# Two transformer layers on one core: block 0's attention logits are exchanged through DRAM in four quarters instead of two halves

## The chip, the cores and the metric

The kernel runs on one core of one Trainium2 chip. The metric is the device time of one execution in microseconds. A core has a matrix engine (TensorE, PE in the profile; PEld is its weight load), a vector engine (VectorE, DVE), a scalar engine (ScalarE, ACT), a general engine (GpSimd, POOL) and a queue engine (SyncE, SP). Transfers between DRAM and on-chip memory are issued from SP, ACT and POOL and are then carried by the core's 16 DMA engines. Each engine works through its own list of instructions strictly in order, and waits on semaphores where an instruction needs another engine's result.

## The reference

The input x is 2048 tokens by 1024 features, bf16. Two layers are applied twice each, alternating, every one with a residual:

```
x = x + A(layernorm(x))      # layer 0
x = x + B(layernorm(x))      # layer 1
x = x + A(layernorm(x))      # layer 2
x = x + B(layernorm(x))      # layer 3
```

A is a dilated sliding-window attention: 32 heads of 32 features, and each token attends to itself and to the tokens 2, 4, ... 14 places earlier, 8 positions in all.

```
qkv    = x @ wqkv                                  # 1024 x 3072
logits = einsum("bhsd,bhswd->bhsw", q, kg) / sqrt(32)   # kg: k shifted by 0, 2, ..., 14
attn   = softmax(where(in range, logits, -1e9))
o      = einsum("bhsw,bhswd->bhsd", attn, vg) ;  A = o @ wo
```

B is a gated unit with hidden width 3584: `h = relu(x @ W_gate) * (x @ W_up)`, then `h @ W_down`.

## The kernel before

The tokens are cut into four blocks of 512 (b = 0 to 3), each of four tiles of 128. TensorE does nothing but the matrix products, in an order that the Python code writes out: `proj(0,b)` (q, k, v of layer 0, block b), `wo(L,b)` (the output product of the attention), `plan_gu` and `plan_down` (the gated unit). Weights come in slabs of 1024 x 512 through a ring of five slots. Every product accumulates in one of eight PSUM banks, and ScalarE or VectorE copies it out.

The order on the other engines comes from a planner, the class Plan. Every step is put at a planned time (`plan.at`, `plan.on_dve`, `plan.chain`), the steps are sorted by that time, and the program is emitted in that order. The planned times only set the order; at run time each engine starts an instruction when its waits are over. The work of VectorE for the attention is one long chain (`plan.chain`), and other VectorE work is slipped in between its links by its due time.

All attention except its matrix products is VectorE work, and it needs two layouts. The projections give features on the 128 partitions and tokens along the row; the attention wants 32 heads x 4 token tiles on the partitions. So q, k and v travel through DRAM (`q_d`, `k_d`, `v_d`; loads L540, stores L404 and L407) and come back as `qhm`, `khm`, `vhm`. Block 0 of layer 0 does this differently for its logits (function `first_logits`, L450 to L529). There q and k stay in the feature layout (`q_fm`, `k_fm`), with the columns of the weights picked so that one partition holds one feature group of one head. For each of the eight chunks c of 128 features the code multiplies q with the shifted k (`mul`, L488, all eight shifts at once for c = 0 to 3) and adds the product to a sum in f32 (`add`, L499). After that the 4 partitions of each head still have to be added up. For this the sums go through DRAM: `turn(h)` stores the sums of four shifts, `lacc`, to `l_d` (L505), and loads them back as `lhm` with the four partitions of a head side by side in one row (L511); `fold(h)` (L525, L526) adds the four up into `L`. For c = 4 to 7 the chunks are done for the first four shifts (h = 0) and then for the last four (h = 1), so that the first half can travel while the second is computed.

After the second fold come the mask (L579), the maximum and its subtraction (L581 to L584), the exponential on ScalarE (L587), the normalisation (L592 to L597), and eight groups of products with v (L605 to L615), each stored by POOL to `o_d` (L616). When all eight are stored, SP loads `oT` from `o_d` (L624), and TensorE can start `wo(0,0)` (L684). In TensorE's order `wo(0,0)` stands behind the first group of the second half of q of block 3 (the hook `("q", 1, 0)`, L793).

Around this chain stands other work of block 0's time. `late_ln(0, 3, 70.0, on_vector=True, norm_at=78.0)` (L846) puts the layer norm statistics of block 3 on VectorE (bn_stats L224, bn_aggr L247); POOL takes the power (L257), ScalarE applies it (L264) and SP issues the transposing DMA into `xnT` (L270). The `xnT` tiles, the two `lacc` and one of the `lhm` tiles share a pool of four buffers (`tpose`, tag "T"); the other `lhm` shares one buffer with `q_fm` and `qhm` (`hm_pool`, tag "q"). Block 3's x is loaded in two DMAs (L837, `n = 2`), and the slabs of `wo` in one DMA each (L676).

On SP the order in the stretch from 59 to 107 us is: vhm part 1, transpose of block 2 (first half), vhm part 2, transpose of block 2 (second half), store of `lacc0`, vhm part 3, load of `lhm0`, vhm part 4, store of `lacc1`, load of `lhm1`, transpose of block 3 (first half), qhm part 1, transpose of block 3 (second half).

Of the kernel before, what the change touches and what calls it, by code (L numbers as in the profile page):

```python
# [30 lines left out]
NG = DH // DG  # L31
FG = P // H


# [6 lines left out]
def _ap(t, off, dims):  # L41
    return bass.AP(tensor=t.tensor, offset=t.offset + off, ap=[list(t.ap[0])] + [list(d) for d in dims])
# [81 lines left out]
def kernel(  # L124
# [11 lines left out]
    nc = tc.nc  # L136
# [11 lines left out]
    wo_v = A_wo.rearrange("(kc p) n -> p kc n", p=P)  # L148
# [6 lines left out]
    dram = ctx.enter_context(tc.tile_pool(name="dram", bufs=1, space=bass.MemoryType.DRAM))  # L155
# [143 lines left out]
    class First:  # L299
# [46 lines left out]
        def turn(self, t):  # L346
            self.tp[t] = [psum.tile([P, KC // 2, P], BF16, tag="acc", name="tp") for h in range(2)]
            for c in range(KC):
                nc.tensor.transpose(self.tp[t][c // 4][:, c % 4, :], self.xn[:, t, c * P:(c + 1) * P], ident[:])
# [100 lines left out]
    def first_logits(st, tm):  # L450
        hold, ready = {}, {}
        now = lambda: 0.0

        def begin():
            hold["q"] = hm_pool.tile([P, KC, BLK], BF16, tag="q", name="q_fm")
            hold["k"] = hm_pool.tile([P, KC, HALO + BLK], BF16, tag="k", name="k_fm")
            nc.gpsimd.memset(hold["k"][:, :, 0:HALO], 0.0)

        def evict(nm, c, acc, t):
            def f():  # L460
                if nm == "q":
# [21 lines left out]
        def mul(c, h):  # L483

            def f():
                w, n = (0, W) if h is None else (W // 2 * h, W // 2)
                pr = at_pool.tile([P, n, BLK], BF16, tag="pr", name=f"prod_{c}", bufs=2)
                nc.vector.tensor_tensor(pr[:], _ap(hold["q"], c * BLK, [[0, n], [1, BLK]]),  # L488
                                        _ap(hold["k"], c * ROW + HALO - DIL * w, [[-DIL, n], [1, BLK]]), op=ALU.mult)
                for i in range(2) if h is None else (h,):  # L490
                    hold[("pr", c, i)] = pr[:, W // 2 * i - w:W // 2 * (i + 1) - w].rearrange("p w (q t) -> p w q t", q=TPB)
            return f

        def add(c, h):
            def f():
                if c == 1:
                    hold[("acc", h)] = tpose.tile([P, TPB, W // 2, P], F32, tag="T", name=f"lacc{h}")
                acc = hold[("acc", h)][:].rearrange("p q w t -> p w q t")
                nc.vector.tensor_tensor(acc, hold[("pr", 0, h)] if c == 1 else acc, hold[("pr", c, h)], op=ALU.add)  # L499
            return f  # L500

        def turn(h):

            def store():
                nc.sync.dma_start(l_d[h].rearrange("q p w t -> p q (w t)"),  # L505
                                  hold[("acc", h)][:].rearrange("p q w t -> p q (w t)"))

            def load():
                pool, tag = ((tpose, "T"), (hm_pool, "q"))[h]
                hold[("l", h)] = pool.tile([P, FG, W // 2, P], F32, tag=tag, name=f"lhm{h}")  # L510
                nc.sync.dma_start(hold[("l", h)][:].rearrange("p a w t -> p (a w t)"),  # L511
                                  l_d[h].rearrange("q (h a) w t -> (q h) (a w t)", a=FG))
# [7 lines left out]
        def fold(h):  # L520
            def f():
                if h == 0:
                    st["L"] = at_pool.tile([P, W, P], F32, tag="L", name="L_0_0")
                l = hold[("l", h)]
                nc.vector.tensor_tensor(l[:, 0:2], l[:, 0:2], l[:, 2:4], op=ALU.add)  # L525
                nc.vector.tensor_tensor(st["L"][:, 4 * h:4 * h + 4, :], l[:, 0], l[:, 1], op=ALU.add)  # L526
            return f

        return {"evict": evict}  # L529
# [143 lines left out]
        return st  # L673

    def plan_wo(L, b, st, done):
        ws = [slab(wo_v[:, :, h * SLAB:(h + 1) * SLAB], f"wo_{L}_{b}_{h}", 30.0) for h in range(2)]  # L676
        hold = {}

        def mms(half, t):
            def f():  # L680
                acc = psum.tile([P, BLK], F32, tag="acc", name="acc_wo")
                hold[(half, t)] = acc
                for c in range(KC):
                    nc.tensor.matmul(acc[:], lhsT=st["oT"][:, c, t, :], rhs=ws[half]["t"][:, c, :],  # L684
                                     start=(c == 0), stop=(c == KC - 1))
            return f

        def add(half, t):
            def f():
                xs = x_tiles[b * TPB + t][:, half * SLAB:(half + 1) * SLAB]  # L690
                nc.vector.tensor_tensor(xs, hold.pop((half, t))[:], xs, op=ALU.add)
            return f

        wo_start.append((L, b, plan.pe, st["tm"]))
        st["wo_at"] = plan.pe
        for t in range(TPB):
            for half in range(2):
                e = plan.on_pe(8, mms(half, t), [ws[half]])
                plan.on_dve(e + T_EV, 0.7, add(half, t), done[t] if half == 1 else None)
# [203 lines left out]
```

## Time and profile before

| | us |
|---|---|
| median of 3 runs | 1619.19 (1618.88 to 1619.46) |
| the profiled execution | 1619.48 |
| its span, first to last instruction | 1617.7 |
| TensorE busy in it | 1610.6 |
| VectorE busy | 1057.0 |
| ScalarE busy | 440.7 |
| POOL busy | 124.9 |
| granted TensorE clock | 1.0 throughout |

The page of the profile lists busy time, a picture of the span in 40 slices, the DMA queues, the chain of work that ended last, and the costliest groups. Beside it stand views that list, for a stretch of time, every instruction of an engine with what ended its idle time ("the timeline"), who waited for whom ("the waits"), and the chain that ended last in order of time. In all of them the columns are start, duration, engine, line of the kernel, operation and tiles; a bracket holds the idle time before and who ended it. For a DMA the duration is that of its issue; its landing comes later.

### The profile page before, as it was taken

To read this page: it belongs to the slowest core of one execution; us is meant where nothing else is said; L and a number is where in the kernel's file an instruction comes from. 1 tells how busy PE (TensorE), PEld (TensorE's weight loads), DVE (VectorE), ACT (ScalarE), POOL (GpSimd) and SP (SyncE) were. 2 spreads that over 40 slices of the span, in tenths; PEclk is the share of its full clock that TensorE was granted. 3 is DMA by queue.
4 is the path that set the end of the run, shared out by engine and by line. 5 is a ranking of instruction groups with operands and counts; after the bars stand their busy time and mean duration, and the time that the engine had idled before them with its cause. 6 is when DMAs were issued, how large, how long until landed. Compare 5 with 4: busy or idle time off the path is not lost.

```text
span 1617.7 us, 19190 instructions
## 1 busy us (share of the span) xinstructions
PE 1610.6 (100%) x7626; PEld 745.1 (46%) x7626; DVE 1057.0 (65%) x1264; ACT 440.7 (27%) x701; POOL 124.9 (8%) x199
## 2 busy tenths in 40 slices
PE   9999999999999999999999999999999999999999
PEld 6444444444444444444444444444444444444444
DVE  6979999989999169860699617986989212211211
ACT  4642511304131241312413241133021311221110
POOL 2211000001011110011101110001000000000000
PEclk9999999999999999999999999999999999999999
DMA  8887787878966997669876699599846655564552
GB/s 253 235 229 155 210 209 199 209 180 223 214 182 199 239 204 199 193 212 231 198 203 195 210 222 223 162 276 226 227 158 199 177 169 163 175 187 152 157 167 67
DMA packets 445162, 319.01 MB, mean 197 GB/s; under 512 B 195696, under 2 KB 437776, under 8 KB 444816
## 3 DMA queue, kind: packets, MB, share of 16 engines
q1 hardware_dynamic: 415904, 285.59, 66.4%
q10 hardware_dynamic: 24368, 23.40, 4.8%
q0 software_dynamic: 4800, 8.80, 1.8%
q8 instruction: 59, 0.97, 0.3%
q14 instruction: 31, 0.25, 0.1%
HBM read 263.86 MB, written 38.15 MB: 187 GB/s over the span
## 4 chain that ended last, share of the span: by engine, by line
PE 92%; DVE 3%; DMA 3%; ACT 1%; issue 1%; POOL 0%; SPq 0%; ACTq 0%; DVEq 0%; POOLq 0%
PE acc_g L714 24%; PE acc_u L714 24%; PE dacc L761 24%; PE acc_wo L684 7%; PE acc_k L390 5%; PE acc_v L390 5%; PE acc_q L390 5%; DVE pvt L605 1%; DMA l_d<-lacc 1%; DVE pvt L613 1%; DMA q_d<-stage_q 0%; DMA x<-in_A_x_dram 0%; DMA k_d<-stage_k 0%; DVE pvt L614 0%; DMA lhm<-l_d 0%
## 5 line engine op out<-in xcount | busy, mean ns | idle before, releaser
L714 PEld LDWEIGHTS <-ring 128*128 128x128 bf16 x3584 | 350.7, 98 | 422.9
L714 PE MATMUL acc_g<-xnT,ring 128*128 128x512 bf16 x1792 | 423.3, 379 | 0.0
L714 PE MATMUL acc_u<-xnT,ring 128*128 128x512 bf16 x1792 | 423.3, 379 | 0.0
L761 PE MATMUL dacc<-ring,hT 128*128 128x512 bf16 (+1 forms) x1820 | 388.2, 376 | 0.0
L729 DVE TENSOR_TENSOR hT<-acc_u,r 128x512 bf16<-128x512 f32 x224 | 154.1, 688 | 316.9 <-PE acc_u L714 312.2
L721 ACT ACTIVATE r<-acc_g 128x512 bf16<-128x512 f32 x224 | 133.4, 596 | 699.5 <-PE acc_g L714 688.0
L761 PEld LDWEIGHTS <-hT 128*128 128x128 bf16 x1820 | 178.1, 98 | 209.0
L390 PEld LDWEIGHTS <-ring 128*128 128x128 bf16 x1152 | 115.6, 100 | 133.0
L605 DVE TENSOR_TENSOR pvt<-a,vhm 128x4096 bf16<-128x4096 bf16 x64 | 146.2, 2285 | 0.2
L564 DVE TENSOR_TENSOR l<-l,pr 128x1024 f32<-128x1024 f32 x112 | 136.8, 1221 | 2.3
L554 DVE TENSOR_TENSOR pr<-qhm,khm 128x4096 bf16<-128x4096 bf16 x56 | 127.9, 2284 | 13.4 <-DMA khm<-k_d 13.4
L769 DVE TENSOR_TENSOR xb<-dacc,xb 128x512 bf16<-128x512 f32 (+1 forms) x49 | 33.2, 680 | 126.8 <-PE dacc L761 126.6
L390 PE MATMUL acc_k<-xnT,ring 128*128 128x512 bf16 x512 | 113.1, 379 | 0.0
L684 PE MATMUL acc_wo<-ring,oT 128*128 128x512 bf16 x512 | 111.8, 379 | 0.2 <-DMA oT<-o_d 0.2
L390 PE MATMUL acc_v<-xnT,ring 128*128 128x512 bf16 x384 | 84.2, 379 | 0.0
L616 POOL DMA_DIRECT2D o_d<-ohm x64 | 35.3, 551 | 623.2 <-DVE ohm L615 609.3
L613 DVE TENSOR_TENSOR pvt<-pvt 128x2048 bf16<-128x2048 bf16 x64 | 78.1, 1221 | 1.4
L684 PEld LDWEIGHTS <-oT 128*128 128x128 bf16 x512 | 50.1, 98 | 60.8 <-DMA oT<-o_d 0.7
L399 ACT CAST stage_q<-acc_q 128x512 bf16<-128x512 f32 x56 | 31.8, 582 | 157.6 <-PE acc_q L390 142.6
L257 POOL TENSOR_TENSOR rstd<-vpe,neg_half 128x2 f32<-128x2 f32 x30 | 32.2, 1074 | 541.8 <-DVE vpe L256 533.2
L564 DVE TENSOR_TENSOR l<-pr 128x1024 f32<-128x1024 bf16 x56 | 68.2, 1218 | 0.6
L264 ACT ACTIVATE xn_all<-xb,nb,rstd 128x1024 bf16<-128x1024 bf16 x48 | 57.7, 1235 | 30.4 <-POOL nb L258 27.9
(83 smaller groups left out, 841.8 us busy)
## 6 DMA issues: line engine op xcount, KB each, us to landing
ring<-in_B_W_gate_dram SPq DMA_DIRECT2D x56, 1024.0 KB, 7.3
ring<-in_B_W_up_dram SPq DMA_DIRECT2D x56, 1024.0 KB, 5.5
ring<-in_B_W_down_dram SPq DMA_DIRECT2D x48, 1024.0 KB, 5.9
ring<-in_A_wqkv_dram SPq DMA_DIRECT2D x26, 1024.0 KB, 5.6
ring<-in_A_wo_dram SPq DMA_DIRECT2D x16, 1024.0 KB, 7.0
vhm<-v_d SPq DMA_DIRECT2D x32, 284.0 KB, 7.6
v_d<-stage_v ACTq DMA_DIRECT2D x32, 256.0 KB, 6.6
o_d<-ohm POOLq DMA_DIRECT2D x64, 128.0 KB, 3.9
```

Source lines behind the costliest of these rows:

```text
L264: nc.scalar.activation(hold["xn"][:, t, :], x_tiles[b * TPB + t][:], ACT.Identity, scale=rstd[:, i:i + 1], bias=nb[:, i:i + 1])
L390: nc.tensor.matmul(acc[:, t0 * P:t1 * P], lhsT=lhsT, rhs=xnT[(L, b)][:, t0:t1, kc, :], start=(kc == 0), stop=(kc == KC - 1))
L554: nc.vector.tensor_tensor(pr[:], st["q"][:], _ap(st["k"], HALO - DIL * w, [[HALO + P, DH], [1, P]]), op=ALU.mult)
L564: nc.vector.tensor_tensor(l[:], pr[:, 0:8] if i == 0 else l[:], pr[:, 8 * i + 8:8 * i + 16], op=ALU.add)
L605: nc.vector.tensor_tensor(tt[:], a_bc, v_sh, op=ALU.mult)
L613: nc.vector.tensor_tensor(tt[:, 0:4], tt[:, 0:4], tt[:, 4:8], op=ALU.add)
L616: nc.gpsimd.dma_start(_dram(o_d[b], g * DG * P, [[DH * P, P], [1, DG * P]]), o[:].rearrange("p d t -> p (d t)"))
L684: nc.tensor.matmul(acc[:], lhsT=st["oT"][:, c, t, :], rhs=ws[half]["t"][:, c, :], start=(c == 0), stop=(c == KC - 1))
L714: nc.tensor.matmul(acc[:], lhsT=w["t"][:, kc, (j % 4) * P:(j % 4 + 1) * P], rhs=xnT[(L, b)][:, :, kc, :], start=(kc == 0), stop=(kc == KC ...
L721: nc.scalar.activation(r[:], hold.pop(("g", j))[:], ACT.Relu)
L729: nc.vector.tensor_tensor(st["hT"][:, j, :], hold.pop(("u", j))[:], hold.pop(("r", j))[:], op=ALU.mult)
L761: nc.tensor.matmul(accs[(t, c0)][:], lhsT=st["hT"][:, j, t * P:(t + 1) * P], rhs=w["t"][:, jl, c0 - half * SLAB:c0 - half * SLAB + n], sta ...
```

## The change

The constant `LQ = 4` replaces the halves by quarters of two shifts each. The sums, the products of chunks 4 to 7, the stores, the loads and the folds of block 0's logits are cut accordingly: twelve 1024-element additions instead of six of 2048 for chunks 1 to 3, sixteen products of 1024 and sixteen additions of 1024 instead of eight and eight of 2048 for chunks 4 to 7, four stores and four loads of 512 KB instead of two and two of 1 MB, four folds of half the size instead of two. The rows of a store become 1024 bytes instead of 2048, those of a load 4096 instead of 8192. The planned place of a load is 4.0 us behind its last addition instead of 2.5, and of a fold 6.0 us instead of 9.5. The loads go to other buffers: `lhm0` to the buffer of `l1`, parts 1 and 2 to the two halves of one tile of the pool "T", part 3 to the buffer of `q_fm`. Block 3's statistics are due at 72.5 instead of 70.0. The two slabs of `wo(0,0)` are loaded in two DMAs each, and block 3's x in four DMAs instead of two.

```diff
+LQ = 4
...
-    l_d = [dram.tile([TPB, P, W // 2, P], F32, name=f"l_d{h}") for h in range(2)]
+    l_d = [dram.tile([TPB, P, W // LQ, P], F32, name=f"l_d{h}") for h in range(LQ)]
...
-                for h in range(2 if c == KC - 1 else 1):
+                for h in range(LQ if c == KC - 1 else 1):
                     for c in range(KC // 2, KC) if h else (c,):
-                        whole = c < KC // 2
-                        plan.chain.append((lambda c=c: ready[c], 2.3 if whole else 1.2, mul(c, None if whole else h), None))
-                        for i in range(2 if whole else 1) if c else ():
-                            plan.chain.append((now, 2.3, add(c, i if whole else h), turn(h) if c == KC - 1 else None))
-                for h in range(2 if c == KC - 1 else 0):
-                    plan.chain.append((lambda h=h: tm[("l_in", h)], 2.0, fold(h),
-                                       (lambda now: tm.__setitem__("logits", now)) if h else None))
+                        parts = range(LQ) if c < KC // 2 else (h,)
+                        plan.chain.append((lambda c=c: ready[c], 0.1 + 0.55 * len(parts), mul(c, parts), None))
+                        for i in parts if c else ():
+                            plan.chain.append((now, 1.2, add(c, i), turn(i) if c == KC - 1 else None))
+                for h in range(LQ if c == KC - 1 else 0):
+                    plan.chain.append((lambda h=h: tm[("l_in", h)], 1.0, fold(h),
+                                       (lambda now: tm.__setitem__("logits", now)) if h == LQ - 1 else None))
...
+                if c == 1 and i % 2 == 0:
+                    hold[("acc", i // 2)] = tpose.tile([P, 2, TPB, n, P], F32, tag="T", name=f"lacc{i // 2}")
+                acc = hold[("acc", i // 2)][:, i % 2].rearrange("p q w t -> p w q t")
...
             def load():
-                pool, tag = ((tpose, "T"), (hm_pool, "q"))[h]
-                hold[("l", h)] = pool.tile([P, FG, W // 2, P], F32, tag=tag, name=f"lhm{h}")
+                if i == 0:
+                    t = at_pool.tile([P, 1, FG, n, P], F32, tag="l1", name="lhm0")
+                elif i == 1:
+                    t = tpose.tile([P, 2, FG, n, P], F32, tag="T", name="lhm1")
+                elif i == 2:
+                    t = hold["l_in"]
+                else:
+                    t = hm_pool.tile([P, 2, FG, n, P], F32, tag="q", name="lhm3")
...
             def after(now):
                 plan.at(now + 0.1, store)
-                plan.at(now + 2.5, load)
-                tm[("l_in", h)] = now + 9.5
+                plan.at(now + 4.0, load)
+                tm[("l_in", i)] = now + 6.0
...
-        ws = [slab(wo_v[:, :, h * SLAB:(h + 1) * SLAB], f"wo_{L}_{b}_{h}", 30.0) for h in range(2)]
+        ws = [slab(wo_v[:, :, h * SLAB:(h + 1) * SLAB], f"wo_{L}_{b}_{h}", 30.0, 2 if L == b == 0 else 1) for h in range(2)]
...
-    for b, n, at in ((1, 4, -5.7), (2, 1, 25.5), (3, 2, 45.0)):
+    for b, n, at in ((1, 4, -5.7), (2, 1, 25.5), (3, 1, 45.0)):
...
-            late_ln(0, 3, 70.0, on_vector=True, norm_at=78.0)
+            late_ln(0, 3, 72.5, on_vector=True, norm_at=78.0)
```

In the program that results, TensorE's order is the same instruction by instruction. On VectorE the second small group of block 2's statistics (L252 to L256) stands in front of the first part's last addition instead of behind the addition of chunk 5; block 3's statistics stand behind the first of the four folds as they stood behind the first of two, and the other three folds follow them. On SP the stretch becomes: vhm part 1, store of part 0, transpose of block 2 (first half), vhm part 2, transpose of block 2 (second half), load of part 0, store of part 1, vhm part 3, load of part 1, vhm part 4, store of part 2, load of part 2, store of part 3, load of part 3, transpose of block 3 (first half), qhm part 1, transpose of block 3 (second half).

More of the change, by code (lines that the diff above doesn't have):

```diff
@@ L479, in evict @@
-                for h in range(2 if c == KC - 1 else 0):
-                    plan.chain.append((lambda h=h: tm[("l_in", h)], 2.0, fold(h),
-                                       (lambda now: tm.__setitem__("logits", now)) if h else None))
-        def mul(c, h):
-            def f():
[L486 to L491, printed above, removed]
+                        parts = range(LQ) if c < KC // 2 else (h,)
@@ new lines, in first_logits, with mul @@
+        n = W // LQ
+        def mul(c, parts):
+            def f():
+                w, m = n * parts[0], n * len(parts)
+                pr = at_pool.tile([P, m, BLK], BF16, tag="pr", name=f"prod_{c}", bufs=2)
+                nc.vector.tensor_tensor(pr[:], _ap(hold["q"], c * BLK, [[0, m], [1, BLK]]),
+                                        _ap(hold["k"], c * ROW + HALO - DIL * w, [[-DIL, m], [1, BLK]]), op=ALU.mult)
+                for i in parts:
+                    hold[("pr", c, i)] = pr[:, n * i - w:n * (i + 1) - w].rearrange("p w (q t) -> p w q t", q=TPB)
@@ L492, in mul, with add @@
             return f
-        def add(c, h):
+        def add(c, i):
             def f():
[L496 to L499, printed above, removed]
+                if c == 1 and i % 2 == 0:
+                    hold[("acc", i // 2)] = tpose.tile([P, 2, TPB, n, P], F32, tag="T", name=f"lacc{i // 2}")
+                acc = hold[("acc", i // 2)][:, i % 2].rearrange("p q w t -> p w q t")
+                nc.vector.tensor_tensor(acc, hold[("pr", 0, i)] if c == 1 else acc, hold[("pr", c, i)], op=ALU.add)
@@ L500, in add, with turn @@
             return f
-        def turn(h):
+        def turn(i):
             def store():
-                nc.sync.dma_start(l_d[h].rearrange("q p w t -> p q (w t)"),
-                                  hold[("acc", h)][:].rearrange("p q w t -> p q (w t)"))
+                nc.sync.dma_start(l_d[i].rearrange("q p w t -> p q (w t)"),
+                                  hold[("acc", i // 2)][:, i % 2].rearrange("p q w t -> p q (w t)"))
             def load():
-                pool, tag = ((tpose, "T"), (hm_pool, "q"))[h]
-                hold[("l", h)] = pool.tile([P, FG, W // 2, P], F32, tag=tag, name=f"lhm{h}")
-                nc.sync.dma_start(hold[("l", h)][:].rearrange("p a w t -> p (a w t)"),
-                                  l_d[h].rearrange("q (h a) w t -> (q h) (a w t)", a=FG))
+                if i == 0:
[6 more added lines that the diff above has]
+                    t = hm_pool.tile([P, 2, FG, n, P], F32, tag="q", name="lhm3")
+                hold["l_in"] = t
+                hold[("l", i)] = t[:, i == 2]
+                nc.sync.dma_start(hold[("l", i)].rearrange("p a w t -> p (a w t)"),
+                                  l_d[i].rearrange("q (h a) w t -> (q h) (a w t)", a=FG))
@@ L514, in after, with fold @@
             def after(now):
                 plan.at(now + 0.1, store)
-                plan.at(now + 2.5, load)
-                tm[("l_in", h)] = now + 9.5
+                plan.at(now + 4.0, load)
+                tm[("l_in", i)] = now + 6.0
             return after
-        def fold(h):
+        def fold(i):
             def f():
-                if h == 0:
+                if i == 0:
                     st["L"] = at_pool.tile([P, W, P], F32, tag="L", name="L_0_0")
-                l = hold[("l", h)]
+                l = hold[("l", i)]
@@ L525, in f @@
                 nc.vector.tensor_tensor(l[:, 0:2], l[:, 0:2], l[:, 2:4], op=ALU.add)
-                nc.vector.tensor_tensor(st["L"][:, 4 * h:4 * h + 4, :], l[:, 0], l[:, 1], op=ALU.add)
+                nc.vector.tensor_tensor(st["L"][:, n * i:n * i + n, :], l[:, 0], l[:, 1], op=ALU.add)
             return f
```

## The prediction

> **What bounds the kernel now.** I read the page first, then TensorE's waits, then the chain in order of time, then the timelines of VectorE and SP from 64 to 101 us. From the page:
>
> ```profile
> PE 1610.6 (100%) x7626; PEld 745.1 (46%) x7626; DVE 1057.0 (65%) x1264; ACT 440.7 (27%) x701; POOL 124.9 (8%) x199
> ```
>
> TensorE is busy all the time. A busy TensorE may still run below its pace, so the pace is checked: 64 matmuls take 13.81 us wherever the chain shows them, 0.216 us each, at a granted clock of 1.0. The list of all that TensorE waited for is short:
>
> ```profile
> PE warm L310 <- POOL neg_half L183: 1.4, 1, 1.4
> PE acc_v L390 <- DMA wqv<-in_A_wqkv_dram: 1.0, 1, 1.0
> PE tp L349 <- DVE xn_all L344: 0.6, 1, 0.6
> PE acc_v L390 <- ACT xnT L352: 0.5, 2, 0.2
> PE acc_wo L684 <- DMA oT<-o_d: 0.2, 1, 0.2
> ```
>
> Four rows are the first 17 us, which the change leaves alone. Only the last touches block 0's attention. Its true size is that of a slip: the 8 matmuls from 149.87 us on end their turn at 149.87 + 8 x 0.216 = 151.60, and the next starts at 151.93, so 0.33 us. The chain shows what leads there:
>
> ```profile
> 82.31 10.75 DMA l_d<-lacc
> 93.13 5.48 DMA lhm<-l_d
> ...
> 146.10 2.38 DMA o_d<-ohm
> 148.68 3.20 DMA oT<-o_d
> 151.93 13.99 PE acc_wo L684 x64
> ```
>
> So block 0's attention is the critical chain, but it reaches TensorE only 0.33 us late. Whatever it gains beyond 0.33 us is worth nothing; whatever it loses, TensorE loses in full. The stretch that the change rewrites, VectorE then SP:
>
> ```profile
> 77.40 1.22 DVE L488 TENSOR_TENSOR prod<-q_fm,k_fm 128x2048 bf16<-128x2048 bf16 x1
> 78.65 2.29 DVE L499 TENSOR_TENSOR lacc<-lacc,prod 128x2048 f32<-128x2048 f32 x1
> 86.28 1.23 DVE L525 TENSOR_TENSOR lhm<-lhm 128x1024 f32<-128x1024 f32 x1 [5.34 <-DMA lhm<-l_d]
> ...
> 98.63 1.23 DVE L525 TENSOR_TENSOR lhm<-lhm 128x1024 f32<-128x1024 f32 x1 [4.46 <-DMA lhm<-l_d]
> 99.89 0.69 DVE L526 TENSOR_TENSOR L<-lhm 128x512 f32<-128x512 f32 x1
> ```
>
> ```profile
> 71.36 1.07 SPq L505 DMA_DIRECT2D l_d<-lacc  x1
> ...
> 79.43 0.34 SPq L511 DMA_DIRECT2D lhm<-l_d  x1
> 81.72 0.54 SPq L540 DMA_DIRECT2D vhm<-v_d  x1
> 82.31 0.84 SPq L505 DMA_DIRECT2D l_d<-lacc  x1
> 93.13 0.34 SPq L511 DMA_DIRECT2D lhm<-l_d  x1
> ```
>
> The last addition ends at 80.94, the last fold at 100.58: 19.6 us, of which VectorE waits 5.34 and 4.46. The two transfers are the length of it, and each load stands on SP until its own store has landed (79.36 and 93.06), with everything behind it on SP standing too.
>
> **VectorE's part.** In chunks 4 to 7 a pair of product and addition now goes from start to start in 3.47 us (67.01, 70.47, 73.94). The quarter pair: product 0.69 (the row of 128x1024 bf16, L614), addition 1.22 (L564, 128x1024 f32), and the same seams as now (+0.04 between them, -0.08 behind): 1.87. Sixteen make 29.9 against 8 x 3.47 = 27.8: +2.1. In chunks 1 to 3, twelve additions at 1.14 (1.22 - 0.08) make 13.7 against six at 2.21 = 13.2: +0.45. The last addition ends 2.6 later, at about 83.6. The first part ends at 61.3 (the first half did at 67.1), the second at 68.8, the third at 76.2.
>
> The last fold shrinks from 1.23 + 0.69 (1.95 with its seam) to 0.69 + 0.42 (the rows of 128x512 and 128x256 f32, L526 and L582; 1.15): -0.8 behind the last landing. The three others (3.5 us together) and block 3's statistics (88.15 to 94.08, 6.0 us) fall between 83.6 and 93.1. They cost nothing as long as part 3 lands after 93.1; if it lands sooner, they are the chain and end 94.3 at best.
>
> **SP's part.** Every transfer is placed behind what stands before it on SP and behind the bytes in front of it. Packets go out about 1.0 us behind an issue; 1 MB of load takes 4.1 to 4.8 (lhm), 1 MB of store 4.7 to 5.3 (l_d), a vhm part 2.0 to 3.1; the landing follows 0.4 to 1.6 behind the last packet.
> - Store 0 at 61.5 is in front of block 2's transpose (63.58) and its issue of about 1 us ends before that. Load 0 follows the second transpose at 71.3, lands about 77.8.
> - Store 1 is ready at 68.8 but shares a semaphore with a k store that landed at 73.04; it lands at about 80. Load 1 waits for it and for a q store (landed 81.71): issued 80.3 to 81.7, landing about 85.5.
> - vhm part 4 and store 2 follow at 82; the bytes of load 1 and vhm go first, to about 86.6; store 2's take 2.6, landing about 90.7 (now: 93.06).
> - Load 2 at 90.8, landing 94.2. Store 3, ready since 83.6, stands behind it and behind a v store (landed 92.47 now, in the shadow of the 1 MB store): about 91.2; its bytes to 95.5, landing 97.
> - Load 3 at 97.1: 1.0 + 2.05 + 0.4, landing 100.5. Last fold to 101.7.
>
> Against 100.58 that is **+1.1 us**: the halved last transfers gain about 8 us, and the load that stands on SP between two stores gives it all back. The 2.6 us of VectorE are hidden in store 3's wait; if SP were free they would be paid.
>
> Bounds, nearest rows however far. A 512 KB transfer costs at least what 256 KB cost (oT 3.20, o_d 128 KB 2.38) and at most what 1 MB cost (store 10.75 and 8.00, load 5.48). Low: vhm part 4 at its fastest (4.35) from 82.1, store 2 two behind it, 88.5; store 3 issued 88.9, + 3.2; load 3 + 3.2, 95.3; fold 96.5: -4.1, of which 0.33 counts. High: store 2 82.6 + 10.75, store 3 + 8.0, load 3 + 5.5, fold: 108.0, +7.4. I take the middle because the two l_d rows split into packets (4.7, 5.3) and waiting (the rest), and only packets halve.
>
> The store's rows get shorter: in this trace a 2048-byte packet takes 94 ns and a 1024-byte one 55, so half the bytes take 58% of the time; it is in the 2.6. The Trainium skill (Perfetto Trace Analysis, DMA Optimizations) says that transfers under 2 KB carry significant overhead, which speaks against the change. The packets agree in direction, at 17% more per byte, 0.25 us a store.
>
> **The rest of the edits.** The `wo` slabs and block 3's x add four issues of about 0.5 us (37 to 47 us); SP is idle from 47.2 to 59.33, so nothing, or 2 us on vhm part 1 without that pause. Their data: landed 55.8 at the latest now, needed at 84.8 (statistics) and 151.9 (`wo`). Block 3's transposes now also wait for TensorE's end of block 1 at 94.6 (the buffer of that `xnT`): they stand behind load 3 anyway, and TensorE needs them at 136.05 against 107.2 now. The exponential stands behind one more q copy, done by 97, before 104. khm part 4, ahead of oT on SP, waits for a later v store (136.99 instead of 134.83); oT is due at 148.7.
>
> **Sum.** Profiled execution 1619.48 (span 1617.7 and 1.8 around it) + 1.1 = 1620.6. The median of the runs is 0.3 below the profiled one: 1620.3.
>
> **The rivals.**
> 1. *Small and early.* The quarters land by 99.1 or sooner (fold by 100.25), and the slip of 0.33 goes, no more: 1618.9. For it: v stores and q stores may land earlier without a 1 MB store before them, which frees SP sooner. Against: VectorE's 2.6 and four legs in a row. The Trainium skill (DMA: Bandwidth & Descriptors, Anatomy of one DMA) gives about 2.0 us plus bytes at 436 GB/s, so 3.2 us for 512 KB, an estimate from its fit; store 3 and load 3 would then end at 97.6 and this rival would hold. The trace's 1 MB legs of 5.48 to 10.75 against its 4.4 speak against that here.
> 2. *The queue does not shrink.* Store 2, load 2, store 3 and load 3 each cost as now, since waiting and not bytes is their length; load 2 holds store 3 on SP. Fold at up to 108.0: 1619.2 + 7.4 = 1626.6. It decides (over 0.2%) once load 3 lands later than about 102.6. For it: store 0 took 8.00 and store 1 10.75 for 4.7 and 5.3 of packets. This is the other side.
> 3. *Another gate.* Block 0's next layer norm lands its second transpose at 190.20, and TensorE needs it at 191.65: 1.5 us of slack, and the change shifts VectorE's order around the `wo` additions. Landing 5 us late would cost 3.5: 1623.8 with the forecast. For it, the transposes' landings of 4.3 to 9.5; against it, they wait on the same delayed chain as TensorE, so the slack travels along, and one chain link fewer stands before the second group.
> 4. *Faster by more than 0.2%.* It would need 3.2 us, and TensorE has 0.33 to give. Nothing in the waits offers it.
>
> **How the numbers follow.** 0.2% is 3.2 us, about what a measurement of this kernel can tell from no change. Chances: forecast (load 3 lands between 99.1 and 102.6) 0.50; rival 1, 0.22; rival 2 beyond its point 0.20; rival 3, 0.06; rival 4, 0.02. Same 0.72, slower 0.26, faster 0.02. Time 1620.3; the range goes from 1618.7 (rival 1 less the spread of runs) to 1624.5 (rival 2 up to two thirds of its price), leaving out some 0.15 above and 0.03 below. The likeliest case alone: 1619.2 to 1622.4.
>
> **What the profile of after would show.** TensorE's wait for oT: about 1.4 (0.33 + 1.1); gone in rival 1; over 3.5 in rival 2; a new row for xnT at 191 in rival 3. Last addition at 83.6, store 1 issued at 73, load 2 at 90.8, store 3 right behind it, load 3 at 97, last fold at 101.7. Wrong would be: store 3 issued near 83.6 (the queue does not hold it) or later than 93.

## The result and the profile after

| | before | after |
|---|---|---|
| median of 5 runs, us | 1619.37 (1618.88 to 1619.97) | 1626.00 (1624.21 to 1627.66) |
| profiled execution, its span | 1619.48, 1617.7 | 1626.86, 1625.2 |
| granted TensorE clock, mean | 1.0 | 0.998 |

The ratio is 1.0040, with a 95% interval of 1.0029 to 1.0050. The change makes the kernel slower by more than the 0.2% that a measurement can tell. Its time lies 5.7 us above the forecast and 1.5 above the range. Three later series of the same kernel (10, 3 and 10 executions) had medians of 1624.25, 1620.10 and 1621.88, all inside the range; the series of the result is the latest of the four. So the spread is a part of the result, and the experiments come back to it.

The busy times of after, from its page:

```profile
PE 1612.0 (99%) x7626; PEld 745.0 (46%) x7626; DVE 1059.6 (65%) x1290; ACT 440.6 (27%) x701; POOL 128.0 (8%) x199
```

VectorE has 2.6 us more to do, as priced, and TensorE has the same instructions but 1.4 us more of busy time. What TensorE waited for in block 0's stretch, from its waits in after (us in total, times, longest):

```profile
PE acc_wo L695 <- DMA oT<-o_d: 5.8, 1, 5.8
...
PE acc_q L391 <- ACT stage_q L400: 0.5, 1, 0.5
```

The wait for oT was 0.2 and the other row is new. The chain of after in order of time (start, duration, what) leads there:

```profile
83.02 8.68 DMA l_d<-lacc
92.14 6.89 DMA l_d<-lacc
99.05 5.38 DMA lhm<-l_d
...
151.12 3.43 DMA o_d<-ohm
154.79 2.87 DMA oT<-o_d
157.70 15.64 PE acc_wo L695 x64
```

Three legs stand where two stood, and `wo(0,0)` starts at 157.70 instead of 151.93: 5.77 of the 7.38 us between the two profiled executions. Its 64 matmuls then take 15.64 instead of 13.99. That is 1.65, and together it makes 7.42. The order of SP is what the change made of it (timeline of SP in after):

```profile
82.05 0.32 SPq L522 DMA_DIRECT2D lhm<-l_d  x1
...
83.02 0.65 SPq L508 DMA_DIRECT2D l_d<-lacc  x1
91.72 0.32 SPq L522 DMA_DIRECT2D lhm<-l_d  x1
92.14 0.38 SPq L508 DMA_DIRECT2D l_d<-lacc  x1
99.05 0.32 SPq L522 DMA_DIRECT2D lhm<-l_d  x1
```

The sums of part 3 are complete at 83.38, as the timeline of VectorE in after shows with the last fold:

```profile
82.16 1.22 DVE L502 TENSOR_TENSOR lacc<-lacc,prod 128x1024 f32<-128x1024 f32 x1
...
104.45 0.69 DVE L536 TENSOR_TENSOR lhm<-lhm 128x512 f32<-128x512 f32 x1 [7.05 <-DMA lhm<-l_d]
105.18 0.42 DVE L537 TENSOR_TENSOR L<-lhm 128x256 f32<-128x256 f32 x1
```

So their store waits 8.8 us on SP: load 2 stands in front of it, and SP may not issue load 2 before store 2 has landed (91.71). A second hold ends at the same moment: store 3 shares a semaphore with a v store that was issued at 84.52 and landed at 91.73. The last fold ends at 105.60, before at 100.58. The longer matmuls are the clock. The windows of after (stretch, length, busy time of PE, PEld, DVE, ACT and POOL with instruction counts, granted PE clock, DMA share, GB/s):

```profile
154.00:158.00 4.00, 0.30 (x1) 0.13 (x2) 3.85 (x5) 0.00 (x0) 0.00 (x0) 0.53 0.56 127
158.00:162.00 4.00, 4.00 (x13) 1.49 (x12) 3.91 (x4) 0.00 (x0) 0.00 (x0) 0.62 1.26 199
162.00:166.00 4.00, 4.00 (x20) 1.82 (x19) 3.90 (x6) 0.00 (x0) 0.00 (x0) 1.00 1.34 153
```

13 matmuls are at work in four microseconds, and 20 in the next four at a clock of 1.0. Eight starts are about 0.427 apart, where the others are 0.216. With a clock of 0.5 or 1.0, the two means put its fall at 154.25, 2.4 us after the last matmul ended (151.89), and its return at 161.1, 3.4 after `wo(0,0)` began. The Trainium skill (TensorE: Matmul & The Clock Gate, What's actually happening) says that an idle window of about 3.4 us halves the clock, that about 3.4 us of work restore it, and that the window runs free of the kernel. The trace agrees on the return, after 3.4 us of work. On the fall it agrees less well: the clock fell 2.4 us into the idle time, and further down waits of 3.0 to 3.35 us are enough.

### The profile page after: what moved, and what is told of

It reads as the page before. It is cut to its first block, busy times and chain, and to the rows that moved or that the text cites. A ratio compares the mean times of both kernels' runs of the same rounds, so it can differ in the third digit from the quotient of the medians.

```text
span 1625.2 us, 19234 instructions
## 1 busy us (share of the span) xinstructions
PE 1612.0 (99%) x7626; PEld 745.0 (46%) x7626; DVE 1059.6 (65%) x1290; ACT 440.6 (27%) x701; POOL 128.0 (8%) x199
## 4 chain that ended last, share of the span: by engine, by line
PE 91%; DVE 5%; DMA 3%; issue 0%; ACT 0%; SPq 0%; POOL 0%; ACTq 0%; DVEq 0%; POOLq 0%
PE acc_g L725 24%; PE acc_u L725 24%; PE dacc L772 24%; PE acc_wo L695 7%; PE acc_v L391 4%; PE acc_k L391 4%; PE acc_q L391 4%; DVE pvt L616 1%; DMA l_d<-lacc 1%; DVE lacc L502 1%; DMA xnT<-xn_all 1%; DVE pvt L624 1%; DVE prod L491 0%; DMA xb<-in_A_x_dram 0%; DVE pvt L625 0%; DMA lhm<-l_d 0%
## 5 line engine op out<-in xcount | busy, mean ns | idle before, releaser
L391 PE MATMUL acc_v<-xnT,ring 128*128 128x512 bf16 x384 | 84.2, 379 | 0.0
L582 DVE TENSOR_TENSOR l<-l 128x512 f32<-128x512 f32 x112 | 62.3, 556 | 3.0
```

Source lines behind the costliest of these rows:

```text
L391: nc.tensor.matmul(acc[:, t0 * P:t1 * P], lhsT=lhsT, rhs=xnT[(L, b)][:, t0:t1, kc, :], start=(kc == 0), stop=(kc == KC - 1))
L582: nc.vector.tensor_tensor(l[:, 0:n], l[:, 0:n], l[:, n:2 * n], op=ALU.add)
```

## The experiments

**The order on SP.** Load 2 is planned later, behind store 3:

```diff
-                plan.at(now + 4.0, load)
+                plan.at(now + (8.5 if i == 2 else 4.0), load)
```

> The changed kernel, with one planned place moved: load 2 stands behind store 3 on SP instead of in front of it (the place of load 2 is 8.5 us behind its last addition instead of 4.0); with that, store 3 shares its semaphore with a k store that landed at 84.9 instead of a v store that landed at 91.7. Theory 'hold': the late chain comes from store 3, ready at 83.4, standing behind load 2 and the v store until 92.14. Then store 3 goes out by about 85, right behind store 2, lands about 93.5, load 3 is issued about 94 and lands about 98; the last fold ends about 99 instead of 105.6, TensorE's wait for oT falls from 5.8 to 0.3 us or less, no matmul runs at half clock, and the time is 1619.0 to 1619.8. Rival 'bytes': four quarters with the v parts between them fill the queue whatever their order; then load 3 lands at 102 or later, the wait for oT stays above 3 us and the time above 1622.5.

Measured: 1619.17 (1618.61 to 1620.25), ratio 1.0000, interval 0.9991 to 1.0009. The timelines of SP and VectorE in this kernel:

```profile
82.21 4.66 SPq L508 DMA_DIRECT2D l_d<-lacc  x2
90.65 1.62 SPq L522 DMA_DIRECT2D lhm<-l_d  x2
```

```profile
97.98 0.69 DVE L536 TENSOR_TENSOR lhm<-lhm 128x512 f32<-128x512 f32 x1 [0.63 <-DMA lhm<-l_d]
98.71 0.42 DVE L537 TENSOR_TENSOR L<-lhm 128x256 f32<-128x256 f32 x1
```

Store 3 is issued at 86.50 (behind a k store of ScalarE with which it now shares a semaphore), lands at 91.88, and the fold ends at 99.13. One planned time takes away the whole loss. But it lifts both holds at once: load 2 no longer stands in front, and store 3 has left the semaphore of the v store, which landed at 90.3 here and would have kept it until then. The ten executions lie within 1.6 us. The wait for oT is gone, so they can't show a gain: TensorE is the bound again.

**One load for two parts.** Parts 2 and 3 keep their own stores but share one load of 1 MB, so that no load can stand between the stores:

```diff
+    l_p = dram.tile([TPB, P, 2, W // LQ, P], F32, name="l_p")
...
-                nc.sync.dma_start(l_d[i].rearrange("q p w t -> p q (w t)"),
+                to = l_d[i] if i < 2 else l_p[:, :, i - 2]
+                nc.sync.dma_start(to.rearrange("q p w t -> p q (w t)"),
...
+                    nc.sync.dma_start(hold[("l", 3)][:].rearrange("p a w t -> p (a w t)"),
+                                      l_p.rearrange("q (h a) j w t -> (q h) (a j w t)", a=FG))
...
```

> The changed kernel with parts 2 and 3 stored one by one but loaded together, 1 MB in rows of 8192 bytes behind store 3, so that no load stands between the two stores. Theory (SP's order holds store 3): store 3 is issued at about 86.5 as when load 2 was put behind it, lands at 92, the load is issued at 92. If a row's price goes by its size (0.45 us for 8192 bytes as before, against 0.29 to 0.34 for 4096), the load lands at 97.0 and the last fold ends at 99; if it goes by the traffic, at 98.4 and 100.4. Time 1619.3 to 1619.7, no half-clock matmuls. Rival (not the order but the store itself is slow): store 3 lands at 96 to 99, the last fold ends at 103 to 106, and the time is 1623 to 1626.

Measured: 1619.74 (1618.95 to 1620.21), ratio 1.0003, interval 0.9993 to 1.0013. SP and VectorE:

```profile
82.81 3.31 SPq L510 DMA_DIRECT2D l_p<-lacc  x2
92.25 0.33 SPq L522 DMA_DIRECT2D lhm<-l_p  x1
```

```profile
98.17 1.23 DVE L541 TENSOR_TENSOR lhm<-lhm 128x1024 f32<-128x1024 f32 x1 [6.11 <-DMA lhm<-l_p]
```

Store 3 goes at 85.75, lands at 92.17, and the load at 98.14; the fold ends at 100.12. That is nearer to the price by traffic than to the one by size of row; but it is the second kernel in which store 3 lands at 92 and nothing is lost. What held store 3 was its place on SP and not the store itself. Here too it shares a semaphore with a k store (landed at 85.69), so these two kernels don't part the two holds; a trace further down does.

**The small edits alone**, the kernel before with them:

```diff
-..., f"wo_{L}_{b}_{h}", 30.0) for h in range(2)]
+..., f"wo_{L}_{b}_{h}", 30.0, 2 if L == b == 0 else 1) for h in range(2)]
-    for b, n, at in ((1, 4, -5.7), (2, 1, 25.5), (3, 2, 45.0)):
+    for b, n, at in ((1, 4, -5.7), (2, 1, 25.5), (3, 1, 45.0)):
-            late_ln(0, 3, 70.0, on_vector=True, norm_at=78.0)
+            late_ln(0, 3, 72.5, on_vector=True, norm_at=78.0)
```

> The kernel before, with the three small edits alone: the slabs of wo(0,0) in two DMAs each, block 3's x in four DMAs, block 3's statistics due at 72.5. Theory (all that was lost is in the quarters): the same within 0.1%, 1619.4, TensorE's wait for oT 0.2 us. Rival (the four more issues, or the other rotation of semaphores that they cause, delay the exchange): a wait for oT of 2 us or more, and 1621.5 or more.

Measured: 1619.50 (1618.91 to 1619.92), ratio 1.0002, interval 0.9992 to 1.0011. They cost nothing, as priced.

**Block 3's transpose behind qhm**, to see whether it lengthens load 3, which it follows on SP:

```diff
-            late_ln(0, 3, 72.5, on_vector=True, norm_at=78.0)
+            late_ln(0, 3, 72.5, lag=6.0, on_vector=True, norm_at=78.0)
```

> The changed kernel, with block 3's first transpose one place later on SP, behind the first qhm load, which itself waits for the last fold; so no transpose is issued while load 3 is under way. Theory 'transpose': load 3 took 5.38 us to land, 3.9 us of it packets, where 0.5 MB at the pace of the last load before the change (1 MB in 4.1 us) would take 2.05, because the transpose was issued 0.4 us behind it. Then load 3 lands 3.5 to 4.0 us after its issue, the last fold ends 1.4 to 1.9 us earlier, the wait for oT falls to about 4, and the time to about 1624.3. Rival 'small load': half a load costs nearly what a whole one costs; then load 3 stays at 5.0 to 5.4 us and the time at 1626.

Measured: 1622.07 (1619.48 to 1624.91), ratio 1.0016, interval 1.0007 to 1.0026. Load 3 took 3.91 instead of 5.38. This looked like an answer, and was none: the next kernel, with the transpose where after has it, had 4.09.

**No idle time ahead of `wo(0,0)`**, 72 matmuls of 128x128 on `ident` whose result is not used:

```diff
+                if L == b == half == t == 0:
+                    scratch = psum.tile([P, P], F32, tag="acc", name="warm")
+                    for i in range(72):
+                        nc.tensor.matmul(scratch[:], lhsT=ident[:], rhs=ident[:], start=True, stop=True)
```

> The changed kernel with 72 matmuls of 128x128 on a constant in front of wo(0,0), which keep TensorE busy for some 4 us of its wait of 5.8 us; their result is not used. Theory 'clock': the 8 matmuls after the wait run at 0.427 instead of 0.216 us because the clock that TensorE is granted falls to half in the idle time (154.2 to 161.1 us in the trace). Then none runs at 0.427, the granted clock is 1.0 throughout, and the time is 1.7 to 1.9 us less, about 1624.2. Rival 'data': they run slowly because oT or the weights arrive slowly; then the 8 stay at 0.427 and the time at 1626.

Measured: 1622.77 (1622.32 to 1623.70), ratio 1.0022, interval 1.0012 to 1.0031. The 72 take 4.0 us, no start is 0.427 apart, and the first part of oT landed at 154.33, before they ended: `wo(0,0)` started at 155.13, right behind them. The clock stays up when TensorE is kept busy, but here the filler was itself the wait. The time is 1.4 below the expectation, which was worked from the late trace of the result; the last fold ended at 101.08 here. The ten executions lie within 1.4 us, which fits a chain that ends under the filler.

**Lateness alone.** The kernel before, with links of block 0's maximum (L581, L582) repeated, which changes no value and no transfer. The shorter one does L581 four times; the longer one is:

```diff
-            nc.vector.tensor_tensor(m[:], Lt[:, 0:4], Lt[:, 4:8], op=ALU.max)
-            nc.vector.tensor_tensor(m[:, 0:2], m[:, 0:2], m[:, 2:4], op=ALU.max)
+            for i in range(8 if L == b == 0 else 1):
+                nc.vector.tensor_tensor(m[:], Lt[:, 0:4], Lt[:, 4:8], op=ALU.max)
+            for i in range(2 if L == b == 0 else 1):
+                nc.vector.tensor_tensor(m[:, 0:2], m[:, 0:2], m[:, 2:4], op=ALU.max)
```

> The kernel before, with the maximum's first link done eight times and its second twice: about 5.6 us more behind the last fold, as late as the changed kernel's last fold is against the start of TensorE's work. Theory (lateness, and behind it the lower clock, are the whole price): wait for oT about 5.9, 8 matmuls at 0.427 behind it, 1619.3 + 5.6 + 1.8 = 1626.7. Without the lower clock: 1624.9. Rival (the transfers' collisions cost something of their own elsewhere): at most 1623.

Measured: 1625.37 (1623.82 to 1626.04), ratio 1.0038, interval 1.0023 to 1.0053. Its waits:

```profile
PE acc_wo L686 <- DMA oT<-o_d: 3.4, 1, 3.4
...
PE acc_q L390 <- ACT stage_q L399: 1.4, 1, 1.4
```

Half-clock starts follow (seven, 1.45 us), and the new small row of after appears too: ScalarE stands at the exponential, which waits for the late fold, the q copies behind it stand, and TensorE runs out of PSUM banks. This delay only uses up part of the wait that comes later. With transfers untouched, lateness alone gives a loss about as large as after's (four executions). It came out 1.3 below the expectation, and the shorter one shows why:

> The kernel before, with only the largest link of the maximum (L581) of block 0, layer 0 done four times instead of once: about 2.2 us more on the chain behind the last fold, no change to a transfer. Theory (lateness alone is the price): wo(0,0) starts 2.2 us later, the wait for oT is 2.3 to 2.6; if an idle time of 2.5 is too short to lower the clock, 1621.5; if it lowers it as 3.0 did, 8 matmuls at 0.427 and 1623.3. Rival (lateness is absorbed, and the loss of the changed kernel comes from its transfers colliding with others): 1619.3 to 1620.

Measured: 1620.45 (1619.47 to 1621.48), ratio 1.0008, interval 0.9998 to 1.0017; wait 0.9 instead of 2.3 to 2.6, no half clock. In these two kernels the last fold ended at 99.33 and 99.57, ahead of the repeated links, and in the one with the small edits at 99.13. That led to a second trace of the kernel before:

> The kernel before, unaltered, for a second trace. In the three other kernels with its halves (the two with extra VectorE work, and the one with only the small edits) the last fold ended at 99.1 to 99.6, against 100.58 in the execution that the prediction was worked from. Theory (that execution was a late one): the fold ends at 99 to 100 and the wait for oT is gone. Rival (those three differ by their edits): 100.4 to 100.8 and the slip of about 0.3 again.

Measured: 1618.48, no wait for oT. VectorE in that trace:

```profile
98.13 0.69 DVE L526 TENSOR_TENSOR L<-lhm 128x512 f32<-128x512 f32 x1
```

The fold ends at 98.82. Of five executions with halves the one that the prediction was worked from, 100.58, is the latest; the five average 99.5.

**The same kernel again**, unaltered. First on one chip with the kernels with late links and with the paired load:

> The changed kernel unaltered, on one chip with the three kernels beside it. If the lateness of the last legs is a fixed cost of the order on SP, the wait for oT is 5.8 again, load 3's leg 5.4 and the time 1626. If a part of it is chance between executions (the same order gave 5.38 for load 3 in this kernel and 4.09 in the one with extra matmuls), load 3's leg lies between 4.1 and 5.4, the wait between 3.5 and 5.8, and the time between 1623 and 1628, with half-clock matmuls behind the wait in all of them.

Measured: 1624.25 (1619.80 to 1626.07), ratio 1.0029, interval 1.0019 to 1.0038. The profiled execution took 1619.80, with a wait of 0.6. So the chance between executions is larger than this expectation had it, and three more traces were taken. The second and third expectations repeat the first in short:

> The changed kernel unaltered, for its trace alone. Two executions of it stand apart so far: in one the four last legs took 8.68, 4.51, 6.89 and 5.38 and the last fold ended at 105.6 (1626.9), in the other 7.42, 4.63, 4.52 and 4.00 and 101.0 (1619.8). Theory (the same order, only the legs' length differs by chance): the fold ends between 101 and 106, and the time follows it at about one for one from 1619.8 at 101.0, with about 1 to 1.7 more for half-clock matmuls where the wait for oT is over 3. Rival (something else differs between the two, the start of TensorE or another wait): time and fold do not go together.

> As the run before: a further trace of the changed kernel, the fold between 101 and 106, the time 1619.8 plus what the fold is later than 101.0, plus 1 to 1.7 where the wait for oT is over 3.

> As the two before: a further trace of the changed kernel, the fold between 101 and 106, the time 1619.8 plus what the fold is later than 101.0, plus 1 to 1.7 where the wait for oT is over 3.

Last, on one chip with the two kernels further down:

> The changed kernel unaltered, on one chip with the two kernels beside it: 18 executions so far gave 1618.97 to 1627.66, median 1624.3. The same spread is expected, median 1623 to 1626. In the trace, where store 3 is issued at least 0.5 ahead of the v store next to it, its leg is 4.4 to 5.5, and where the v store is ahead, over 6.

Measured: 1621.88 (1619.32 to 1624.17), ratio 1.0018, interval 1.0008 to 1.0027. The median lies below the 1623 expected, and store 3's leg of 5.60 just above its 5.5. All six traces, against the prediction's chain:

| trace | store 3 issued | landed | load 3 landed | last fold ends | last o_d store took | `wo(0,0)` starts | time |
|---|---|---|---|---|---|---|---|
| predicted | 91.2 | 97 | 100.5 | 101.7 | as before | 153.0 | 1620.6 |
| after | 92.14 | 99.03 | 104.43 | 105.60 | 3.43 | 157.70 | 1626.86 |
| after_again | 91.32 | 95.84 | 99.86 | 101.03 | 2.41 | 152.28 | 1619.80 |
| after_b | 90.63 | 95.03 | 99.01 | 100.19 | 2.43 | 151.45 | 1618.97 |
| after_c | 90.57 | 96.05 | 100.79 | 101.97 | 3.15 | 154.45 | 1623.66 |
| after_d | 90.92 | 95.87 | 100.07 | 101.24 | 2.29 | 152.58 | 1620.10 |
| after_e | 91.00 | 96.60 | 101.06 | 102.23 | 2.91 | 154.25 | 1621.77 |

Store 3 is issued right behind load 2 (0.42 after it) in after, after_c and after_e; in the other three it stood 1.0 to 1.2 us longer, for the v store that shares its semaphore. In the first three that v store had landed only 0.1 to 0.4 us before the issue. So without load 2 in front, but on the same semaphore, store 3 could have gone at most 0.4 us sooner in any of the six, as the landings stand.

The time less the start of `wo(0,0)` is 1467.52 in four of them, as it was before (1619.48 - 151.93 = 1467.55), and 1469.16 and 1469.21 in after and after_c. So the start of `wo(0,0)` and the clock account for the time of every execution. The chain of after_b, the quickest, to be held against that of after:

```profile
84.56 6.01 DMA v_d<-stage_v
...
90.63 4.39 DMA l_d<-lacc
95.04 3.97 DMA lhm<-l_d
...
145.72 2.43 DMA o_d<-ohm
...
148.38 3.02 DMA oT<-o_d
151.45 13.99 PE acc_wo L695 x64
```

And the same 64 matmuls in after_e and in after_c (timeline of PE; the bracket is the idle time before them):

```profile
154.25 13.99 PE L695 MATMUL acc_wo<-ring,oT 128*128 128x512 bf16 x64 [2.59 <-DMA oT<-o_d]
```

```profile
154.45 15.67 PE L695 MATMUL acc_wo<-ring,oT 128*128 128x512 bf16 x64 [3.35 <-DMA oT<-o_d]
```

A start 0.20 later costs 1.9 us. In all traces waits of up to 2.6 kept the clock, and waits of 3.0 or more lost it, at 1.5 to 1.7 us. No sharp limit follows: in after the clock fell 2.4 us into the wait, and after_e's wait of 2.6 kept it.

**Why the legs differ.** In after a v store of ScalarE was issued at 91.80, 0.34 ahead of store 3, which took 6.89; in the five others the v store came 1.0 to 1.3 behind, and store 3 took 4.39 to 5.60. Two kernels were to test whether that order makes a leg long. Both let ScalarE copy half of a stage onto itself three times; in the one ahead of the last two v stores:

```diff
+                for i in range(3 if (L, b, nm, g) == (0, 1, "v", 1) else 0):
+                    nc.scalar.copy(s[:, 1, :], s[:, 1, :])
```

> The changed kernel, with ScalarE copying half a stage onto itself three times (about 1.5 us) ahead of the last two v stores of block 1, so that they are issued later. Theory (a leg is long where a v store was issued ahead of it, and each long leg lets the next v store get ahead): store 3 and load 3 are always ahead of their v stores, legs at most 5.0 and 4.3, last fold by 101.3, time 1619 to 1620.5 in nearly all executions, no half-clock matmuls. Rival (the legs' spread is not a matter of order): the spread of the changed kernel, 1619 to 1627, median 1623 to 1625.

Measured: 1623.92 (1619.88 to 1625.27), ratio 1.0025, interval 1.0015 to 1.0035. In its trace the v stores come 2.8 behind both, and still store 3 took 5.69, the fold ended at 102.80 and the wait was 3.2. The spread is that of after. The theory falls. This trace also parts the two holds. Store 3 shares its semaphore with a k store here, which landed at 84.9, and its sums were ready at 84.2; still it goes only behind load 2 (timeline of SP):

```profile
91.37 0.32 SPq L524 DMA_DIRECT2D lhm<-l_d  x1
91.79 0.38 SPq L510 DMA_DIRECT2D l_d<-lacc  x1
```

So load 2 in front is enough to hold store 3, and with the v store's hold gone the loss stays. In after_b it was the v store's landing that came last (1.6 us behind load 2's issue), so that is enough too.

The other kernel has the copies ahead of the q store that load 1 waited for:

```diff
+                for i in range(3 if (L, b, nm, g, j) == (0, 1, "q", 1, 3) else 0):
+                    nc.scalar.copy(s[:, 1, :], s[:, 1, :])
```

> The changed kernel, with the same three copies ahead of the q store that load 1 waits for through a shared semaphore, so that the chain on SP comes about 1.5 us later while the v stores stay: store 3 is issued at 92 to 93, behind the v store of 91.8 to 92.4. Theory (order): store 3's leg is 6 to 7 and load 3's 4.7 to 5.4, the last fold ends at 104 to 106.5, the wait for oT is over 4, the time 1625 to 1628 in nearly all executions. Rival (not the order): legs of 4.4 to 5.5 and 4.0 to 4.7, the fold no more than 1.5 later than the 100.2 to 102.0 of the four faster traces, and the spread as in the changed kernel.

Measured: 1621.13 (1618.85 to 1627.80), ratio 1.0018, interval 1.0006 to 1.0030. It did not do what it was for: in the new order load 1 no longer waited for that store and was issued at 79.89, as store 1 landed, and the chain came earlier, not later (store 3 at 89.25, fold at 100.17). It tells nothing of the order, only that an earlier chain keeps the spread. Store 3 lands 1.5 to 1.6 us behind load 2 in five of the six traces, whenever it was issued, and 2.8 behind in after. Of the 5.4 us by which after's last fold is later than after_b's, 2.7 are there when store 2 lands, 1.3 come with store 3 and 1.4 with load 3. What makes the same legs 8.4 us together in one execution (after_b) and 12.3 in another (after) stays open.

## Why the prediction was wrong

**TensorE's bound, the edits, VectorE.** Right. The last addition ended at 83.38 (83.6), the small edits are free, and no wait at xnT (rival 3) appeared.

**SP's part.** Right as a mechanism and as an average, too short for the execution of the result. That store 3 stands "behind it and behind a v store" is what the traces show: the load "that stands on SP between two stores" is enough to hold it, the v store's semaphore is too, and the two kernels that lift both lose nothing. The kernel with the later v stores lifts the semaphore alone and loses as after does; no run lifts the load alone. Over six traces the last fold ends at 102.0 on average, against 101.7; store 3 was issued at 91.1 and load 3 landed at 100.9, against 91.2 and 100.5. That this average fits is partly luck, since two errors cancel in it: store 3 landed at 96.4 (97), and load 3 took 4.5 (3.4). In the traced execution of the result each leg was longer than its term: store 2 8.68 (about 8.1), store 3 6.89 (5.8), load 3 5.38 (3.4). The fold came 3.9 us later than forecast, and that is the larger part of the 6.3 us by which this execution missed 1620.6. Load 3 was too short a term throughout: 3.97 to 5.38, never 3.4. Halving 4.1 us of packets did not hold: load 3's packets ran for 2.7 to 3.9 us from the first to the last. One of them took 0.29 us on average in after (0.30 to 0.34 in loads 1 and 2) and 0.25 to 0.28 in the other five, against 0.44 to 0.49 for the 8192-byte ones before. The base was short too: the first load's packets before ran from 80.45 to 85.86, 5.4 us, where the prediction has 4.1 to 4.8. The estimate from the Trainium skill (DMA: Bandwidth & Descriptors, Anatomy of one DMA), 3.2 us for 512 KB, fell with it and holds for none of these legs. The page's fit is for transfers issued from GpSimd, and these are issued from SP. Rival 1's fold by 100.25 came once in six.

**"Whatever it loses, TensorE loses in full."** This is the step whose mechanism failed, and the rest of the miss, 2.4 us. TensorE loses more than the chain does, in two places that the prediction gave no price. After_c shows it without the late legs: its fold ended at 101.97, 0.3 from the forecast, and its time was 1623.66, 3.1 above the forecast for the profiled execution.
- Behind the fold. It took the 51.35 us from fold to `wo(0,0)` as fixed. They were 51.25 to 51.34 in the three early traces, and 52.0 to 52.5 in the late ones, because the last store to `o_d` took 2.9 to 3.4 instead of 2.3 to 2.4. It goes with a k store of ScalarE, which is issued at 146.7 to 147.5 (149.35 and 150.94 in after): in the six traces of all 17 where the `o_d` store is issued less than 0.2 us ahead of a k store, or behind it, it took 2.9 to 3.4, and in the eleven where it is further ahead, 2.2 to 2.5, even at 150.63 in the longer of the late kernels. So in these traces it is the place against the k store that counts, not the time. This is read from the traces, and no run moved the one store alone. The Trainium skill (DMA: Bandwidth & Descriptors, Queues, rings and completion order) says that each DMA engine takes turns between the queues by packets; the longer store fits that.
- Behind the wait. In every trace with a wait of 3.0 us or more the clock fell, and 1.5 to 1.7 us came on top.

So rival 2's point of decision, "once load 3 lands later than about 102.6", was wrong. There is no such point: after_e, which landed at 101.06, is 2.3 us above the profiled execution of before, and after_c, which landed at 100.79, is 4.2 above it: 1.4 for the later fold, 0.8 for o_d (3.15 against 2.38), 0.3 for oT (3.53 against 3.20) and 1.7 for the clock. Rival 2's full price, 7.4 for a fold at 108.0, was reached by after with a fold at 105.6: 5.0 for the fold, 0.75 behind it and 1.65 for the clock.

**One execution taken for the kernel.** The slip of 0.33 was read from the latest of five executions with halves; the usual slack is about 1 us. With it, the halves' own spread (fold 98.8 to 100.6) hardly reaches TensorE: 1618.3 to 1620.3 over 25 executions. The quarters' chain is 2.5 us later on average (102.0 against 99.5), has no slack, and its spread goes into the time, in one direction only: 28 executions from 1618.97 to 1627.66, their median 1623.6 (ten on one chip span 1619.80 to 1626.07, so it is not only the chip). A forecast that adds up one value for each leg gives about the quick end of that (1620.3). In 17 of the 28 the time is more than 0.2% above 1619.2, where the prediction gave "slower" 0.26.

No kernel here beats the one before. With the order mended the quarters tie with it, since TensorE has next to nothing to give.

## What to carry to other kernels

Ahead of an engine that is always busy, take a chain's slack from several executions, and price a change that uses it up by the spread of the chain and not by its mean: what comes early is worth nothing and what comes late is paid. If a wait of the matrix engine can grow to about 3 us, add the matmuls at half clock behind it. When transfers are cut into parts, write down the issue queue in order and look for a part's load that must wait for its own store: it holds every store behind it. Look also at which semaphores the stores share: here one planned time mended it because it moved store 3 off a late semaphore as well.

## What the runs showed that was not expected

- Lateness feeds itself: after_c's last fold ends 0.73 later than after_d's, its `wo(0,0)` starts 1.87 later, and its time is 3.56 longer.
- One program took 8.4 to 12.3 us for the same two transfers of 512 KB, while TensorE's work behind `wo(0,0)` took 1467.52 us to a hundredth, the clock aside.
- Three short copies on ScalarE changed which transfer shared a semaphore with which, and so moved load 1 forward by 0.9 to 2.2 us (79.89 against 80.82 to 82.05): what a small edit does to such sharing can be larger than the edit.
